# One Strassen pair for the q projection of two row chunks, in a transformer block on one Trainium2 core

## The chip, the cores and the metric

The kernel runs on one core of a Trainium2 chip. Five engines work side by side, each through its own list of instructions in order: TensorE (PE in the profile, with its weight loads as PEld), VectorE (DVE), ScalarE (ACT), GpSimd (POOL) and SyncE (SP). In this kernel SP issues most of the DMAs, POOL those of attention, and ACT a few. The metric is the device time of one execution in microseconds (us). The kernel before takes 770.53 us (median of 7 runs, 770.19 to 772.18).

## The reference

Input x has S = 2048 rows of D = 1024. Part A is a layer norm, a projection to q, k and v (1024 to 3 x 1024), a sliding attention with 32 heads of 32 (each row looks at 8 keys, two rows apart), an output projection, and a residual. Part B is a layer norm, two projections g and u to 3584, their product, and a projection down, with a residual. All data are bf16.

```python
qkv = layernorm(x) @ wqkv                  # q, k, v of 32 heads x 32
idx = pos[:, None] - 2 * arange(8)[None]   # keys s, s-2, ... s-14; before the start: masked
logits = einsum("bhsd,bhswd->bhsw", q, k[idx]) * 32 ** -0.5
o = einsum("bhsw,bhswd->bhsd", softmax(logits), v[idx])
h = x + o @ wo
n = layernorm(h)
out = h + ((n @ w_gate) * (n @ w_up)) @ w_down
```

## The kernel before

The rows are cut into four chunks of 512 (TC), numbered 0 to 3. Activations that feed a matmul are kept transposed: lnT of chunk c holds the normalised rows as 128 partitions x 8 blocks (KO) x 512. A projection group is eight matmuls of 128x128 by 128x512 into one PSUM tile. The pool of PSUM has 8 tiles.

The projection weights come in six blocks of 512 columns: blocks 0 and 1 are q, 2 and 3 are k, 4 and 5 are v. `qkv(c, blocks)` (L434) runs four groups for each block; after each group `evac_qkv` (L342) copies the PSUM tile to a staging tile on ScalarE and SP stores it to DRAM (qd, kd, vd), so that attention can load it in another layout. k and v also copy a halo of 16 rows.

Attention of one chunk (`attention`, L468) is work for VectorE: products of q and k for eight shifts, adds over the head's 32 entries, the softmax (its exponential on ScalarE), products with v, adds. It needs q and k loaded by POOL (`load_qk`, L448, L451 and L452), then v (`load_v`). At its end POOL stores o to DRAM (L536) and loads it back transposed in four parts (L539), one for each 128 rows; wo reads part t for its rows t. The four attentions run one after the other.

TensorE's order is the order of the program text. Everything else is put in between by a planner, `Background` (L37): after each group `bg.step(1.73)` adds that many microseconds of credit (times `bg.rate`, at most 4.0 in hand), and as long as credit is above zero the planner emits the next piece of the first item on its list that is due; the piece gives back its estimated VectorE time, which is taken off. An item can also ask to be called again later, which costs no credit. `bg.spend` takes credit off for VectorE work that the program emits itself, and `bg.finish` emits the rest of an item at once. Items are attention, the layer norms (`rows_gen` on VectorE for chunks 1 and 2; `NormOnScalar`, L259, on ScalarE for chunk 3), and the absolute sums of half of w_down (`abs_down`, L664: seven pieces of 128x2048 on ScalarE, each from a ring tile that ACT's queue loads), which are needed later for f16 scaling.

The stage around the change (L875 to L903): projections of chunk 0 (q, k), of chunk 1 (q, k), v of chunks 0 and 1, all of chunk 2, q and k of chunk 3; then `wo_ln2(0)` (L589), which runs the output projection of chunk 0 in eight groups, adds the residual on VectorE (L604), takes the row statistics there (L183, L184) and normalises there (L192), with the transposes on SP (L596); then v of chunk 3; then the FFN of chunk 0 (`ffn1_first`, L694), in the middle of which the output projection of chunk 1 is run by `wo_norm` (L569, matmuls L578, adds L580), whose layer norm is on ScalarE (`Norm2`, L550: sums L274, mean L277, squares L279, rstd L282 to L285, rows L296).

Weights of 1 MB stream through seven tiles (`wpool`): `pump` loads the next ones in order while fewer than seven are held, and `retire(n)` lets go of n and pumps. The ring of `abs_down` is one of the seven.

The FFN of chunks 2 and 3 is already done as Strassen pairs (`pair_block`, L829, matmuls L826): the two chunks and the two halves of the contraction, against two column blocks, give a 2x2 by 2x2 block product in seven products in place of eight. The sums of weights are in f16, scaled by a power of two that `Scale` (L628) takes from the absolute sums of the weights. The products are accumulated in PSUM, and ScalarE copies a partial sum from one PSUM tile to another (L843, L851) wherever two results share it.

## Time and profile before

| what | us |
|---|---|
| median of 7 runs | 770.53 (770.19 to 772.18) |
| the profiled execution's own time | 770.42 |
| its span, first to last instruction | 768.6 |
| TensorE busy | 763.1 (99%) |
| VectorE busy | 606.2 (79%) |
| ScalarE busy | 512.7 (67%) |
| wo of chunk 0, first matmul | 163.50 |
| FFN of chunk 0, first matmul | 191.13 |
| wo of chunk 1, first matmul | 253.29 |

The page gives busy time by engine, then the span in 40 slices of 19.2 us (a digit is the busy share in tenths), then the chain of work that ended last. A line of a list by time has start, duration, engine, line of the kernel, operation, output <- input, count, and in brackets the idle time before it with what ended it. A duration can be longer than the distance to the next instruction of the same engine, since neighbours overlap at their ends; where a sum over one engine is made, the distance from start to start is used. Granted TensorE clock is 1.00 throughout.

### The profile page before, as it was taken

To read this page: it belongs to the slowest core of one execution; us is meant where nothing else is said; L and a number is where in the kernel's file an instruction comes from. 1 tells how busy PE (TensorE), PEld (TensorE's weight loads), DVE (VectorE), ACT (ScalarE), POOL (GpSimd) and SP (SyncE) were. 2 spreads that over 40 slices of the span, in tenths; PEclk is the share of its full clock that TensorE was granted. 3 is DMA by queue.
4 is the path that set the end of the run, shared out by engine and by line. 5 is a ranking of instruction groups with operands and counts; after the bars stand their busy time and mean duration, and the time that the engine had idled before them with its cause. 6 is when DMAs were issued, how large, how long until landed. Compare 5 with 4: busy or idle time off the path is not lost.

```text
span 768.6 us, 10302 instructions
## 1 busy us (share of the span) xinstructions
PE 763.1 (99%) x3663; PEld 350.8 (46%) x3663; DVE 606.2 (79%) x718; ACT 512.7 (67%) x979; POOL 142.0 (18%) x152
## 2 busy tenths in 40 slices
PE   8999999999999999999999999999999999999998
PEld 6444444444444444444444444444444444444444
DVE  5629999999999999999998997975454444568863
ACT  4648966423687398778899986836777677788240
POOL 0000000200002000020000001018778677600000
PEclk9999999999999999999999999999999999999999
DMA  7999796999966689579559448574342423730001
GB/s 269 272 252 264 202 281 148 274 314 273 308 217 214 218 294 297 169 256 323 188 187 298 140 155 284 120 199 106 80 110 55 110 76 90 256 127 29 0 29 55
DMA packets 190915, 144.85 MB, mean 188 GB/s; under 512 B 81808, under 2 KB 181136, under 8 KB 188688
## 3 DMA queue, kind: packets, MB, share of 16 engines
q1 hardware_dynamic: 180416, 116.94, 53.8%
q0 software_dynamic: 3584, 22.02, 8.5%
q10 hardware_dynamic: 6864, 5.24, 2.4%
q8 instruction: 28, 0.46, 0.3%
q14 instruction: 23, 0.19, 0.1%
HBM read 110.10 MB, written 27.26 MB: 179 GB/s over the span
## 4 chain that ended last, share of the span: by engine, by line
PE 97%; DVE 2%; DMA 0%; issue 0%; ACT 0%; DVEq 0%
PE ps L431 21%; PE dx L944 6%; PE py L826 6%; PE pwu L431 6%; PE pg L431 6%; PE pz L826 6%; PE px L826 6%; PE pwg L431 6%; PE pu L431 6%; PE wo L998 4%; PE pv L826 3%; PE ez L944 3%; PE ey L944 3%; PE ex L944 3%; PE dy L944 3%; PE wo L578 2%
## 5 line engine op out<-in xcount | busy, mean ns | idle before, releaser
L431 PE MATMUL ps<-lnT,w_qkv 128*128 128x512 bf16 x736 | 159.5, 379 | 0.0
L431 PEld LDWEIGHTS <-w_qkv 128*128 128x128 bf16 x736 | 71.9, 98 | 86.1 <-issue 0.2
L344 ACT CAST sg<-ps 128x512 bf16<-128x512 f32 x96 | 55.1, 586 | 46.5 <-PE ps L431 41.1
L477 DVE TENSOR_TENSOR prod<-qD,kD 128x4096 bf16<-128x4096 bf16 x32 | 72.2, 2285 | 13.1 <-DMA kD<-kd 13.0
L523 DVE TENSOR_TENSOR pv<-vD,at 128x4096 bf16<-128x4096 bf16 x32 | 72.4, 2286 | 0.2
L826 PEld LDWEIGHTS <-sw 128*128 128x128 f16 x448 | 43.8, 98 | 52.9 <-issue 0.2
L431 PEld LDWEIGHTS <-w_wg 128*128 128x128 bf16 x448 | 43.8, 98 | 52.9
L431 PEld LDWEIGHTS <-w_wu 128*128 128x128 bf16 x448 | 43.8, 98 | 52.9
L826 PE MATMUL px<-lnT,ws 128*128 128x512 bf16 x224 | 55.2, 379 | 0.0
L536 POOL DMA_DIRECT2D od<-oD x4 | 2.2, 542 | 276.0 <-DVE oD L534 276.0
L431 PE MATMUL pu<-lnT,w_wu 128*128 128x512 bf16 x224 | 52.9, 379 | 0.0
L431 PE MATMUL pg<-lnT,w_wg 128*128 128x512 bf16 x224 | 52.9, 379 | 0.0
L431 PE MATMUL pwg<-lnT,w_wg 128*128 128x512 bf16 x224 | 52.9, 379 | 0.0
L431 PE MATMUL pwu<-lnT,w_wu 128*128 128x512 bf16 x224 | 52.9, 379 | 0.0
L826 PEld LDWEIGHTS <-ws 128*128 128x128 f16 x336 | 32.9, 98 | 39.6
L807 POOL TENSOR_TENSOR sw<-ws 128x512 f16<-128x512 f16 x26 | 30.0, 1154 | 82.8 <-PE pv L826 49.1
L944 PEld LDWEIGHTS <-gs 128*128 128x128 f16 (+1 forms) x280 | 27.4, 98 | 33.0
L479 DVE TENSOR_TENSOR prod<-prod 128x4096 bf16<-128x4096 bf16 x16 | 36.6, 2289 | 0.4
L843 ACT COPY py<-px 128x512 f32<-128x512 f32 x28 | 16.0, 570 | 28.6 <-PE px L826 28.6
L808 POOL TENSOR_TENSOR sw<-sw,ws 128x512 f16<-128x512 f16 x26 | 30.0, 1153 | 2.0
L810 POOL TENSOR_TENSOR sw<-ws,sw 128x512 f16<-128x512 f16 x26 | 30.0, 1154 | 0.0
L809 POOL TENSOR_TENSOR sw<-ws 128x512 f16<-128x512 f16 x26 | 30.0, 1153 | 0.0
(334 smaller groups left out, 1473.1 us busy)
## 6 DMA issues: line engine op xcount, KB each, us to landing
w_wg<-in_B_w_gate_dram SPq DMA_DIRECT2D x14, 1024.0 KB, 7.2
w_wu<-in_B_w_up_dram SPq DMA_DIRECT2D x14, 1024.0 KB, 6.4
w_pair<-in_B_w_gate_dram SPq DMA_DIRECT2D x14, 512.0 KB, 3.9
w_pair<-in_B_w_up_dram SPq DMA_DIRECT2D x14, 512.0 KB, 5.2
w_wo<-in_A_wo_dram SPq DMA_DIRECT2D x6, 1024.0 KB, 7.3
w_qkv<-in_A_wqkv_dram SPq DMA_DIRECT2D x5, 1024.0 KB, 11.3
kd<-sg SPq DMA_DIRECT2D x32, 144.0 KB, 4.3
kD<-kd POOLq DMA_DIRECT2D x4, 1152.0 KB, 8.4
```

Of the source, the lines that this page charges most:

```text
L344: nc.scalar.copy(sg[:, HB:HB + TC], ps[:])
L431: nc.tensor.matmul(ps[:], lhsT=wt[:, ko, bass.ts(j, 128)], rhs=rhs[:, ko, :], start=(ko == 0), stop=(ko == KO - 1))
L477: nc.vector.tensor_tensor(prod[:, j], qD[:], kD[:, :, o:o + SUB], ALU.mult)
L479: nc.vector.tensor_tensor(prod[:, :, 0:16], prod[:, :, 0:16], prod[:, :, 16:32], ALU.add)
L523: nc.vector.tensor_tensor(pv[:, j], vD[:, :, o:o + SUB], at[:, w, None, :].to_broadcast((128, DH, SUB)), ALU.mult)
L807: eng.tensor_tensor(sw[:, i, 0], a21, a22, ALU.add)
L808: eng.tensor_tensor(sw[:, i, 1], sw[:, i, 0], a11, ALU.subtract)
L809: eng.tensor_tensor(sw[:, i, 2], a11, a21, ALU.subtract)
L810: eng.tensor_tensor(sw[:, i, 3], a12, sw[:, i, 1], ALU.subtract)
L826: nc.tensor.matmul(ps[:], lhsT=lhs[:, ko, :], rhs=rhs[:, ko, :], start=(fresh and ko == 0), stop=(ko == 3), skip_group_check=not fresh)
L944: nc.tensor.matmul(ps[:, bass.ds(lo, n)], lhsT=lhs[k][:, bass.ts(q, 128)], rhs=rhs[k][:, bass.ds(lo, n)], start=(fresh and k == 0), stop=( ...
L998: nc.tensor.matmul(ps[:], lhsT=oTs[c][:, kk, t, :], rhs=wts["wo", 2, hf][:, kk, :], start=(kk == 0), stop=(kk == KO - 1))
```

## The change

q of chunks 2 and 3 is no longer computed by `qkv`. Blocks 0 and 1 of the weights stay in their tiles, and after wo of chunk 0 two calls of `q_pair` compute q of both chunks by seven products each for two column groups (of four). For that:

- The absolute sums of the q weights are taken during the first projections (`q_abs`, two on VectorE, two on ScalarE), one small matmul gives the scale, `q_convert` turns the two weight tiles into f16 in place, and `q_weight_sums` forms sixteen sums of weights. Since the tiles are then f16, q of chunk 1 is computed from them and scaled back in its copy.
- q of chunk 1 moves behind its k; q of chunks 2 and 3 leaves the row of projections, so wo of chunk 0 comes eight groups earlier, with v of chunk 3 ahead of it.
- `q_row_sums` forms sums of the transposed activations on VectorE, in between the adds of wo.
- In `q_pair` ScalarE makes the copies between PSUM tiles and the results of chunk 2; VectorE the results of chunk 3.
- The norm of chunk 0 after wo moves from VectorE to ScalarE, by `wo_norm(0, devs=False)`: sum and squares of each row tile in one step, the last of them, the rstd and the four rows as an item of the planner during the pair.
- q and k of chunk 0 are loaded only when the normalised rows of chunk 1 have landed (a one-element copy on POOL that reads them). The rows of chunk 3 are loaded when k of chunk 0 has landed (again by such a copy), and stand on SP ahead of two weight blocks and the transposes of chunk 2. The norm of chunk 3 is one item, due 14 us after k of the first half of chunk 1.
- `abs_down` is due 52 us after that point in place of 25 after an earlier one.
- The planner is charged 6.0 in place of 8.0 before wo. Attentions 2 and 3 are started after the pair.

The f16 view `f16` and the class `Scale` move up in the text unchanged, and `wo_ln2` is gone.

```diff
+    def f16(ap):
+        return ap.bitcast(F16)
...
-    def load_x(c, what, eng):
+    def load_x(c, what, eng, after=None):
         tiles = []
         for t in range(4):
             xt = hp.tile([128, D], BF, tag="h", name=f"{what}{c}_{t}")
+            if after is not None and t == 0:
+                nc.gpsimd.tensor_copy(xt[:, 0:1], after)
...
+            self.rstds()
+
+        def rstds(self):
...
+        def both(self):
+            yield from self.sums()
+            yield from self.rows()
...
+    scale_q = Scale("q", 4)
...
-        nc.scalar.copy(sg[:, HB:HB + TC], ps[:])
+        if c == 1 and m < 8:
+            nc.scalar.activation(sg[:, HB:HB + TC], ps[:], ACTF.Copy, scale=scale_q.inv)
+        else:
+            nc.scalar.copy(sg[:, HB:HB + TC], ps[:])
...
+                if (b, j) in at:
+                    at[b, j]()
                 ps = psum.tile([128, TC], F32, tag="mm", name=f"ps{c}_{b}_{j}")
-                mm_group(ps, wts["qkv", b], j, lnTs[c])
+                wt = wts["qkv", b][:]
+                mm_group(ps, f16(wt) if c == 1 and b < 2 else wt, j, lnTs[c])
...
-    def load_qk(c):
+    def load_qk(c, after=None):
         qD = att.tile([128, DH, SUB], BF, tag="qD", name=f"qD{c}")
         kD = att.tile([128, DH, SUB + HB], BF, tag="kD", name=f"kD{c}")
+        if after is not None:
+            nc.gpsimd.tensor_copy(qD[:, 0, 0:1], after)
...
+        def sum_dev(self, t):
+            col = slice(t, t + 1)
+            self.sum(t)
+            nc.scalar.activation(self.nm[:, col], self.s[:, col], ACTF.Copy, scale=-1.0 / D)
+            nc.scalar.activation(self.junk[:], self.xs[t][:], ACTF.Square, bias=self.nm[:, col],
+                                 accum_out=self.ss[:, col])
+
+        def finish(self, devs=True):
+            if devs:
+                yield from self.devs()
+            else:
+                yield "later", 2.0
+                self.sum_dev(3)
+                yield "later", self.pace
+                self.rstds()
+                yield "later", self.pace
             yield from self.rows()
...
-                if hf == 0 and t > 0:
+                if hf == 0 and t > 0 and devs:
                     n.sum(t - 1)
+                if hf == 1 and t > 0 and not devs:
+                    n.sum_dev(t - 1)
...
+    qsum = {}
+
+    def q_abs(k):
+        src = wts["qkv", k // 2][:, bass.ts(k % 2, 4), :]
+        if k < 2:
+            nc.vector.tensor_reduce(scale_q.l1[:, k:k + 1], src, mybir.AxisListType.XY, ALU.add,
+                                    apply_absolute_value=True)
+        else:
+            scale_q.add(k, src, att.tile([128, 4, 512], BF, tag="oT", name=f"junk_q{k}")[:])
+
+    def q_weight(r, kh, m):
+        return f16(wts["qkv", r][:, bass.ts(kh, 4), bass.ts(m, 128)])
+
+    def q_convert():
+        for r in range(2):
+            wt = wts["qkv", r]
+            nc.vector.tensor_scalar(f16(wt[:]), wt[:], scale_q.s, None, ALU.mult)
+        bg.spend(2.6)
+        bg.add(q_weight_sums(), bg.now)
+
+    def q_weight_sums():
+        for m in range(4):
+            a11, a12, a21, a22 = (q_weight(r, kh, m) for r in range(2) for kh in range(2))
+            if m < 2:
+                rooms = [f16(hp.tile([128, D], BF, tag="h", name=f"qs{m}_{i}")[:]) for i in range(2)]
+                s1, s2, s3, s4 = (r[:, bass.ts(i, 512)].rearrange("p (k c) -> p k c", k=4) for r in rooms
+                                  for i in range(2))
+            else:
+                s1, s2, s3, s4 = (t1k.tile([128, 4, 128], F16, tag="t1k", name=f"qs{m}_{i}")[:] for i in range(4))
+            nc.vector.tensor_tensor(s1, a21, a22, ALU.add)
+            nc.vector.tensor_tensor(s2, s1, a11, ALU.subtract)
+            nc.vector.tensor_tensor(s3, a11, a21, ALU.subtract)
+            nc.vector.tensor_tensor(s4, a12, s2, ALU.subtract)
+            qsum[m] = (s1, s2, s3, s4)
+            yield 1.7
+
+    def q_row_sums():
+        lo, hi = slice(0, 4), slice(4, 8)
+        b11, b21, b12, b22 = (lnTs[c][:, ks, :] for c in (2, 3) for ks in (lo, hi))
+        t1, t2, t4 = ([t1k.tile([128, TC], F16, tag="t1k", name=f"qt{i}_{k}")[:] for k in range(4)] for i in (1, 2, 4))
+        t3 = f16(b12)
+        for k in range(4):
+            nc.vector.tensor_tensor(t1[k], b12[:, k, :], b11[:, k, :], ALU.subtract)
+            nc.vector.tensor_tensor(t2[k], b22[:, k, :], t1[k], ALU.subtract)
+            if k % 2:
+                yield 1.7
+        for k in range(4):
+            nc.vector.tensor_tensor(t4[k], b21[:, k, :], t2[k], ALU.subtract)
+        yield 1.7
+        nc.vector.tensor_tensor(t3, b22, b12, ALU.subtract)
+        yield 1.3
+
+        def cells(t):
+            return [t[:, k, :] for k in range(4)]
+
+        qsum["b"] = (cells(b11), cells(b21), t1, t2, cells(t3), t4, cells(b22))
+
+    def q_product(ps, lhs, rhs, fresh):
+        for ko in range(4):
+            nc.tensor.matmul(ps[:], lhsT=lhs[:, ko, :], rhs=rhs[ko], start=(fresh and ko == 0), stop=(ko == 3),
+                             skip_group_check=not fresh)
+        bg.step(GROUP_US / 2)
+
+    def q_pair(m0, room):
+        b11, b21, t1, t2, t3, t4, b22 = qsum["b"]
+        two, inv = range(2), scale_q.inv
+
+        def bank(k, i):
+            return psum.tile([128, TC], F32, tag="mm", name=f"q{k}{m0 + i}")
+
+        def stage(c, m):
+            return t1k.tile([128, HB + TC], BF, tag="t1k", name=f"sg{c}_{m}")
+
+        def out_scalar(c, m, ps):
+            sg = stage(c, m)
+            nc.scalar.activation(sg[:, HB:HB + TC], ps[:], ACTF.Copy, scale=inv)
+            store_q(c, m, sg)
+
+        def out_vector(c, m, ps, p5):
+            sg = stage(c, m)
+            nc.vector.scalar_tensor_tensor(sg[:, HB:HB + TC], ps[:], inv, p5, ALU.mult, ALU.add)
+            bg.spend(0.75)
+            store_q(c, m, sg)
+
+        xb, yb, zb, ub, p5 = [[None] * 2 for _ in range(5)]
+        sw = [qsum[m0 + i] for i in two]
+        a11, a12, a21, a22 = ([q_weight(r, kh, m0 + i) for i in two] for r in range(2) for kh in range(2))
+        for i in two:
+            xb[i] = bank("x", i)
+            q_product(xb[i], a11[i], b11, True)
+            yb[i] = bank("y", i)
+            nc.scalar.copy(yb[i][:], xb[i][:])
+        for i in two:
+            v = bank("v", i)
+            q_product(v, sw[i][0], t1, True)
+            p5[i] = room[:, m0 + i, :]
+            nc.scalar.activation(p5[i], v[:], ACTF.Copy, scale=inv)
+            q_product(yb[i], sw[i][1], t2, False)
+            zb[i] = bank("z", i)
+            nc.scalar.copy(zb[i][:], yb[i][:])
+        for i in two:
+            q_product(zb[i], sw[i][2], t3, False)
+            ub[i] = bank("u", i)
+            nc.scalar.copy(ub[i][:], zb[i][:])
+            out_vector(3, 4 + m0 + i, zb[i], p5[i])
+            q_product(xb[i], a12[i], b21, False)
+            out_scalar(2, m0 + i, xb[i])
+        for i in two:
+            q_product(ub[i], a22[i], t4, False)
+            out_scalar(2, 4 + m0 + i, ub[i])
+            q_product(yb[i], sw[i][3], b22, False)
+            out_vector(3, m0 + i, yb[i], p5[i])
+
+    qkv(0, [1, 2], at={(1, 1): lambda: q_abs(0), (1, 2): lambda: q_abs(2), (1, 3): lambda: q_abs(1),
+                       (2, 0): lambda: q_abs(3), (2, 2): scale_q.rows})
+    qkv(0, [3], at={(3, 2): scale_q.total, (3, 3): q_convert})
+    load_qk(0, after=lnTs[1][:, 0, TC - 1:TC])
+    start_attention(0)
+    qkv(1, [2])
     bg.finish(rows2)
+    xtiles[3] = load_x(3, "x", nc.sync, after=qkv_in["k", 0][:, 0, 0:1])
+    pump(6)
+    state["live"] += 1
     for t in range(4):
         norm1[2].transpose(t)
-    xtiles[3] = load_x(3, "x", nc.sync)
-    pump(6)
-    state["live"] += 1
-    bg.add(norm1[3].sums(), bg.now + 18.0)
-    start_attention(0)
+    bg.add(norm1[3].both(), bg.now + 14.0, first=True)
     sums = abs_down()
-    bg.add(sums, bg.now + 25.0, first=True)
-    qkv(1, range(4))
+    bg.add(sums, bg.now + 52.0, first=True)
+    qkv(1, [3, 0, 1])
     qkv(0, range(4, 6))
     load_v(0)
-    bg.add(norm1[3].rows(), bg.now, first=True)
     qkv(1, range(4, 6))
     start_attention(1)
     pump(pair_at)
-    qkv(2, range(6))
-    start_attention(2)
+    qkv(2, range(2, 6))
     hss[0] = load_x(0, "h", nc.sync)
-    qkv(3, range(4), last=True)
+    qkv(3, range(2, 6), last=True)
     bg.finish(atts[0])
     bg.rate = 1.03
-    bg.spend(8.0)
-    nxt = wo_ln2(0)
-    qkv(3, range(4, 6), last=True)
+    bg.spend(6.0)
+    state["live"] += 1
+    rows_q = q_row_sums()
+    bg.add(rows_q, bg.now, first=True)
+    norm2 = [wo_norm(0, devs=False)]
+    bg.finish(rows_q)
+    room_q = wpool.tile([128, 4, TC], F32, tag="w", name="room_q")
+    norm2.append(norm2[0].finish(devs=False))
+    bg.add(norm2[1], bg.now, first=True)
+    for m0 in (0, 2):
+        q_pair(m0, room_q)
+    bg.finish(norm2[1])
+    retire(3)
+    lnT2_0 = norm2[0].lnT
+    start_attention(2)
     start_attention(3)
     norm2 = []
 
@@ -911,12 +1042,9 @@
         norm2.append(n.finish())
         bg.add(norm2[1], bg.now, first=True)
 
-    hT0 = ffn1_first(nxt[0], {(4, 2): wo_1})
+    hT0 = ffn1_first(lnT2_0, {(4, 2): wo_1})
```

## The prediction

> **What bounds the kernel now.** I read the page first (busy times, slices, chain), then the chain in order of time, then the lists of single engines around the stages that the change touches. The page, busy times and chain by engine:
>
> ```profile
> PE 763.1 (99%) x3663; PEld 350.8 (46%) x3663; DVE 606.2 (79%) x718; ACT 512.7 (67%) x979; POOL 142.0 (18%) x152
> ...
> DVE  5629999999999999999998997975454444568863
> ACT  4648966423687398778899986836777677788240
> ...
> PE 97%; DVE 2%; DMA 0%; issue 0%; ACT 0%; DVEq 0%
> ```
>
> TensorE (PE) carries 97% of the chain, so removed matmuls are time, and every stall put in between is time too. VectorE (DVE) is full from about 58 to 365 us: whatever is added there makes attention later. The chain in order of time:
>
> ```profile
> 27.09 136.41 PE ps L431 x632
> 163.50 13.81 PE wo L602 x64
> 177.31 13.81 PE ps L431 x64
> 191.13 1.73 PE pg L431 x8
> ```
>
> 136.41/632 = 0.2158 us per matmul, without a hole. The end that matters is 191.13, where the first FFN matmul starts; behind it both kernels do the same matmuls. VectorE's and GpSimd's lists, merged by time:
>
> ```profile
> 52.49 4.50 DVE L477 TENSOR_TENSOR prod<-qD,kD 128x4096 bf16<-128x4096 bf16 x2 [13.04 <-DMA kD<-kd]
> ...
> 134.44 2.29 DVE L534 TENSOR_TENSOR oD<-oD,pv 128x4096 bf16<-128x4096 bf16 x1
> ...
> 155.31 1.23 DVE L484 TENSOR_TENSOR t<-prod 128x1024 f32<-128x1024 bf16 x1
> ...
> 172.49 1.28 DVE L604 TENSOR_TENSOR h<-wo,h 128x512 bf16<-128x512 f32 x2
> ```
>
> ```profile
> 44.01 0.54 POOL L452 DMA_DIRECT2D kD<-kd  x1 [12.34 <-DMA kd<-sg]
> ...
> 137.03 0.54 POOL L536 DMA_DIRECT2D od<-oD  x1 [47.22 <-DVE oD L534]
> 141.93 3.54 POOL L539 DMA_DIRECT2D oT<-od  x4 [4.37 <-DMA od<-oD]
> ```
>
> Attention 0 waits 13.0 us for its k, then runs on VectorE without a hole of note from 52.49 to 136.73; the start of k's load sets all of it. The first wo add (172.49) comes 9 us after wo's first matmul because attention 1 was emitted ahead of it. ScalarE's (ACT) list gives the prices:
>
> ```profile
> 124.61 1.91 ACT L635 ACTIVATE w_ring<-w_ring 128x2048 bf16<-128x2048 bf16 x1
> ...
> 257.50 1.06 ACT L274 ACTIVATE njunk<-h 128x1024 bf16<-128x1024 bf16 x1 [2.97 <-DVE h L580]
> ...
> 270.75 1.15 ACT L279 ACTIVATE njunk<-h,nroom 128x1024 bf16<-128x1024 bf16 x1
> ...
> 551.16 0.57 ACT L851 COPY pz<-py 128x512 f32<-128x512 f32 x1 [0.17 <-PE py L826]
> ```
>
> Start to start on ScalarE: a sum over a row tile 1.05, its tiny mean 0.24, a square 1.15 (270.75 to 271.89); a normalised row 1.15 (280.84 to 281.97); one down sum 1.91 (124.61 to 126.52); a plain PSUM copy 0.48, a scaled one 0.59.
>
> **The change, part by part.**
>
> *Matmuls.* q of chunks 2 and 3 took 2 x 8 x 8 = 128 matmuls; seven products of 4 for each of 4 column groups are 112. Saved: 16 x 0.2158 = 3.45. The kernel has this block already: the Strassen pair blocks (L826) show 0.86 per 4 matmuls and stand in the chain without a hole, f16 weights against bf16 activations. Added: one 64-column matmul for the q scale. The like matmuls of the other scales, 512 wide, leave gaps of 0.2 to 0.3 in the chain (474.84 to 475.05); I take 0.1, between 0.03 and 0.3.
>
> *q row sums, conversion, weight sums.* Four sums over 128x2048. Two go to ScalarE at 1.91 each; they push the issue of the two chunk-1 transposes from 29.64 to about 31.7. The second of these landed 7.7 us after issue at 38.8, with q's load of 1 MB beside it, and TensorE needs it at 38.9. The change holds that load back until the transposes have landed; the others landed 3.4 to 3.8 after issue, so I expect 33.1 + 3.8 = 37. Price 0; if it takes 7.7 again, 40.8, it costs 1.9. Two go to VectorE. No such reduction is in the trace; by size it lies between the 2048-element bf16 add (1.23) and four bn_stats (4 x 0.64 = 2.56), and I take 2.3, the 2 x 1.2 of a 1024-element f32 add. VectorE is idle from 18.00 to 20.43 and from 22.83 to 24.96, exactly where they land, so at 2.3 they cost attention nothing, and at 2.56 about 0.4 us of a row that is not yet due. [...] Conversion is 2 x 1.28 (128x4096), the weight sums 16 x 0.34 (14 f16 subtractions of 512 took 4.78): 8.0 us from about 40, done by 48.5, under the 13 us wait for k. Without that cover all 8.0 would fall on attention 0.
>
> *k's load, x3, SP's queue.* The last k store follows ScalarE, about 1.5 us later than now, so kD is issued at 45.5 instead of 44.0. (On POOL only qD and kD stand behind the new copy that waits for the transposes, and nothing until 88 behind the one that waits for kD.) It landed in 8.4 beside four transposes and x3. These now stand behind it, and the same-sized vD load at 88.24 took 6.4, od (1024 KB) 4.6. I take 5.8: landing at 51.3 against 52.4, so attention 0 is 1.1 earlier (bounds 4.6 and 8.4: 2.3 earlier to 1.5 later). SP now waits for kD before x3, and behind x3 stand the two w_qkv loads, the chunk-2 transposes and the k stores of chunk 1. w_qkv 4 was issued at 49.1 and took 11.3; now about 54.5 + 11.3 = 65.8, needed at 66.6. Price 0, upper end 2. ScalarE's chunk-3 sums wait for ln tiles held by those transposes, some 2 us, covered by eight PSUM banks (8 x 1.73 = 13.8 us). Chunk 3's transposes now stand among chunk 0's last v stores on SP; the last is issued near 84.4, lands in 3.0, so vD is loaded at 88 as now (88.24) and lands 6.4 later, at 94.6, needed at 100. Price 0.
>
> *wo earlier.* Eight projection groups less stand ahead of wo(0): it starts at 163.50 - 13.81 + 0.1 = 149.8. Its first transposed output landed at 141.9 + 5.5 = 147.4; with attention 0 1.1 earlier, 146.3. 3.5 us in hand.
>
> *VectorE at wo.* Following the planner's credits by hand to the 76th group, attention 1 has been given all but the last adds of its second block, so VectorE reaches the first wo add where L484 at 155.31 ends now, 156.6, less 1.1: 155.5. The q row sums (12 x 0.34 and one of 128x2048, 1.2) are emitted from the sixth add on; the part that v needs is done at about 165, when v is due at 165.3, the last (t3) near 168, z at 168.8: price 0 here, and 1:1 once VectorE is later than 157. Chunk 0's statistics (4 x 2.0) leave VectorE; 16 small subtractions and eight PSUM outputs (0.67 each) come: about 2.7 net, so attention 1 ends near 240 instead of 237.0. Its wo starts at 253.3 and the first oT landed at 248.2, so 2 us remain.
>
> *ScalarE at wo and in the pair.* Here the gain goes. Four sum-and-square steps of 2.44 (9.8), two down sums that the new due time puts at 162 and 174 (3.8), the small rstd group (1.33), four rows (4.6): 19.5, besides 24 copies (12.8), between 156.8 and the pair's end. In order of emission: adds of row 0 done at 156.8; sums 0, 1, 2 to 164.2; sixth down sum to 166.1; only then the first x-to-y copy, 166.7. TensorE's y0 could start at 166.2: stall 0.55. Then p5, z0, the fourth sum-and-square (168.1 to 170.6), p5, z1 copy to 171.8: z1 product stalls 0.76. u0 copy behind the rstd group: 0.08. Row 0 and the seventh down sum delay an output: the second pair's v stalls 0.14; row 1 ahead of its first copy: y0 stalls 1.35; rows 2 and 3: 0.11 and 0.49. Together 3.5.
>
> *End of the pair.* Row 3 is done at 184.9; its transpose landed in 3.2 at 185.9 and in 8.1 at 282.1. So 188.1 to 193.0 against 191.3: price 0, upper end 1.7.
>
> **Sum.** 770.42 (profiled execution: span 768.6 and 1.8 around it; 0.1 under the median 770.53) - 3.45 + 0.1 + 3.5 = 770.6. The FFN starts at 191.3, where it starts now.
>
> **The rivals.**
>
> *Faster: ScalarE keeps up.* If the two down sums fall into the gaps of wo rather than into the pair, the same row of stalls shrinks to z1 0.76, u0 0.08, z1 0.18: 1.0, time 770.42 - 3.35 + 1.0 = 768.1. For it: ScalarE was idle 2 to 3 us at a time in wo(1) (2.97 at 257.50). Against it: the planner's credit is below zero there, -7 after the finish of attention 0 and the charge of 6, so it cannot emit them. Without any stall: 767.1.
>
> *Slower: k lands late.* kD needs 8.4 as now: landing 53.9, wo's adds from 158.1, and every microsecond after 154.9 goes one for one into the first y copy. 770.42 - 3.35 + 2.93 + 3.2 = 773.2. It decides beyond 772.1, that is k landing later than 52.8. For it: SP's stores run beside it. Against: x3, weights and transposes no longer do.
>
> *A transfer is late.* The chunk-1 transpose, w_qkv 4, or chunk 0's last transpose: 1 to 2 us each, 771.6 to 772.6.
>
> *VectorE ends attention 1 too late.* 240 + 11.2 (od issue to first oT, as now) = 251.2 against 253.5; an od store of 4 more us costs 2: 772.6.
>
> **How the numbers follow.** About 0.2% (1.5 us) is what a measurement of this kernel tells from no change. Forecast (769.0 to 772.1): 0.42. ScalarE keeps up, below 769.0: 0.24. Late k: 0.18; late transfer: 0.10, half of it over 772.1; attention 1 late: 0.06. Faster 0.24; same 0.42 + 0.05 = 0.47; slower 0.18 + 0.05 + 0.06 = 0.29. The range goes from 768.0 (rival, 768.1) to 774.0 (late k with one late transfer); the forecast alone 769.0 to 772.1.
>
> **What would show it.** Matmuls 3663 - 15; the FFN's first matmul near 191.3; waits of TensorE on ScalarE's copies between 163 and 191 that add up to 3.5, the largest at the second pair's y0; kD landing near 51.3; first wo add near 155.5; w_ring sums inside the pair. I am wrong if TensorE shows no waits there (faster), or waits before 150 or at 253 (slower).

## The result, and the profile after

The changed kernel takes 774.83 us (median of 17 runs, 771.85 to 778.71) where the kernel before takes 770.67 on the same chips: a ratio of 1.005, 95% interval 1.0035 to 1.0065. The prediction was 770.6, its range 768.0 to 774.0. The change is slower, by about 4 us.

These runs fall into groups by the TensorE clock that was granted. Seven are at 1.000 and lie at 771.9 to 773.2; ten are at 0.998 or 0.996 and lie at 774.4 to 778.7. The kernel before was at 1.000 in all eleven executions whose clock is listed with the first set of experiments. (The trace of sums32 below has a granted clock of 0.57 over 4 us and 1.00 on both sides, which makes 3.4 us at half clock. One such window costs 1.7 us, 0.2% of 773, so 0.998 fits one and 0.996 two.) So two things are to be explained: 2.6 us at full clock, and the lower clock.

The profiled execution is one at full clock: 773.08 us, span 771.3 (before: 770.42, span 768.6). Its page, busy times, slices and chain by engine:

```profile
PE 761.7 (99%) x3648; PEld 349.3 (45%) x3648; DVE 625.8 (81%) x750; ACT 535.5 (69%) x1013; POOL 145.1 (19%) x154
...
DVE  6789999989999999999998999885554444568863
ACT  4755957589677398778899985836777676788240
...
PE 64%; DVE 20%; ACT 9%; DMA 4%; issue 2%; ACTq 0%; SPq 0%; DVEq 0%; POOLq 0%
```

TensorE has 3648 matmuls, 15 fewer, as meant, but it no longer carries the chain alone: 97% has become 64%. From the first FFN matmul back, the chain now runs through ScalarE in the pair, then through VectorE's attention 1 and attention 0. TensorE's own list shows where it waits (start, time, in brackets the idle time before and what ended it):

```profile
150.98 13.99 PE L648 MATMUL wo<-w_wo,oT 128*128 128x512 bf16 x64 [1.20 <-DMA oT<-od]
...
167.78 1.02 PE L939 MATMUL qy<-qt,qs 128*128 128x512 f16 x4 [0.22 <-ACT qy L971]
...
173.09 1.02 PE L939 MATMUL qz<-lnT,qs 128*128 128x512 f16 x4 [0.84 <-ACT qz L979]
...
182.41 1.02 PE L939 MATMUL qy<-qt,qs 128*128 128x512 f16 x4 [1.16 <-ACT qy L971]
...
187.38 1.02 PE L939 MATMUL qz<-lnT,qs 128*128 128x512 f16 x4 [0.34 <-ACT qz L979]
...
192.56 1.89 PE L482 MATMUL pg<-lnT,w_wg 128*128 128x512 bf16 x8
...
501.76 10.52 PE L1072 MATMUL ez<-t,a22r 128*128 128x512 f16 x48 [1.02 <-DVE hsr L789]
```

Three places: the first output projection waits 1.20 for the first transposed output of attention 0; the pair waits four times for ScalarE's copies; and at 501.76, deep in the output of the first layer, TensorE waits 1.02 for VectorE. None of the three is in the kernel before. Between the pair's first matmul (164.80) and the first FFN matmul (192.56) lie 27.76 us, of which 28 products take 24.17 (28 x 0.8633), so the pair loses 3.6: the 2.56 in brackets, 0.17 more at each of the four (the brackets count from the end of the last matmul, the sum from start to start), and 0.4 in three gaps that are too small for a bracket.

ScalarE's list in the pair shows why, and GpSimd's list shows the loads and stores of attention:

```profile
165.26 1.90 ACT L362 ACTIVATE w_ring<-w_ring 128x2048 bf16<-128x2048 bf16 x1
167.06 0.19 ACT L362 ACTIVATION_READ_ACCUMULATOR w_ring<-w_ring 128x1 f32 x1
167.15 1.05 ACT L971 COPY qy<-qx 128x512 f32<-128x512 f32 x2
...
177.60 1.90 ACT L362 ACTIVATE w_ring<-w_ring 128x2048 bf16<-128x2048 bf16 x1
...
180.63 1.24 ACT L304 ACTIVATE ln<-h,nroom,rs 128x1024 bf16<-128x1024 bf16 x1
181.77 0.59 ACT L971 COPY qy<-qx 128x512 f32<-128x512 f32 x1
```

```profile
46.07 0.54 POOL L508 DMA_DIRECT2D kD<-kd  x1 [8.62 <-DMA kd<-sg]
...
92.45 0.53 POOL L513 DMA_DIRECT2D vD<-vd  x1 [37.99 <-DMA vd<-sg]
...
136.57 0.54 POOL L592 DMA_DIRECT2D od<-oD  x1 [42.56 <-DVE oD L590]
144.43 3.54 POOL L595 DMA_DIRECT2D oT<-od  x4 [7.32 <-DMA od<-oD]
```

Two down sums of 1.90 stand in the pair ahead of copies that TensorE waits for, as forecast. A new fact is in the last line: the store of attention 0's output was waited for 7.32 us (before: 4.37), and the first transposed output landed at 150.98, where TensorE was ready at 149.78.

| step, us | before | forecast | after |
|---|---|---|---|
| load of k issued | 44.01 | 45.5 | 46.07 |
| attention 0 starts | 52.49 | 51.3 | 52.12 |
| load of v issued | 88.24 | 88 | 92.45 |
| output of attention 0 stored | 137.03 | 135.9 | 136.57 |
| first wo matmul | 163.50 | 149.8 | 150.98 |
| first wo add on VectorE | 172.49 | 155.5 | 156.01 |
| first FFN matmul (chain) | 191.13 | 191.3 | 192.72 |
| span | 768.6 | 768.8 | 771.3 |

The 2.7 us of span are 1.6 up to the first FFN matmul and the wait of 1.0 near 501. The chain in order of time shows what sets the 1.6:

```profile
151.28 2.30 DVE prod L535
...
156.01 1.29 DVE h L650 x2
...
157.32 1.16 ACT njunk L279 x2
...
165.35 1.40 ACT w_ring L362
...
167.25 0.96 ACT qy L971 x2
...
186.74 0.60 ACT qz L979
...
187.38 1.02 PE qz L939 x4
```

VectorE is in attention 1 until 156.01, only then makes the first add of wo, and ScalarE works from 157.32 to the pair's last copies with hardly a pause. The wait of 1.20 at wo(0) is not on this chain: had TensorE been on time there, it would have waited 1.2 longer for the first of ScalarE's copies. In this execution, then, the 1.6 come by way of ScalarE, and the wait at wo(0) would count only if it were longer.

### The profile page after: what moved, and what is told of

Same layout as the page of the kernel before. It is cut to its first block, busy times and chain, and to the rows that moved or that the text cites. A ratio compares the mean times of both kernels' runs of the same rounds, so it can differ in the third digit from the quotient of the medians.

```text
span 771.3 us, 10350 instructions
## 1 busy us (share of the span) xinstructions
PE 761.7 (99%) x3648; PEld 349.3 (45%) x3648; DVE 625.8 (81%) x750; ACT 535.5 (69%) x1013; POOL 145.1 (19%) x154
## 4 chain that ended last, share of the span: by engine, by line
PE 64%; DVE 20%; ACT 9%; DMA 4%; issue 2%; ACTq 0%; SPq 0%; DVEq 0%; POOLq 0%
PE dx L1072 6%; PE px L831 6%; PE pwg L482 6%; PE pu L482 6%; PE py L831 6%; PE pz L831 6%; PE pwu L482 6%; PE pg L482 6%; DVE prod L533 3%; PE pv L831 3%; DVE pv L579 3%; PE dy L1072 3%; DMA b21r<-in_B_w_down_dram 2%; DVE prod L535 2%; PE wo L648 2%; PE wo L1126 2%
## 5 line engine op out<-in xcount | busy, mean ns | idle before, releaser
L482 PE MATMUL ps<-lnT,w_qkv 128*128 128x512 bf16 x608 | 131.7, 379 | 0.0
L482 PEld LDWEIGHTS <-w_qkv 128*128 128x128 bf16 (+1 forms) x608 | 59.3, 98 | 70.9
L396 ACT CAST sg<-ps 128x512 bf16<-128x512 f32 x72 | 41.7, 586 | 27.1 <-PE ps L482 14.6
```

Of the source, the lines that this page charges most:

```text
L396: nc.scalar.copy(sg[:, HB:HB + TC], ps[:])
L482: nc.tensor.matmul(ps[:], lhsT=wt[:, ko, bass.ts(j, 128)], rhs=rhs[:, ko, :], start=(ko == 0), stop=(ko == KO - 1))
```

## The experiments

**Theory at the start.** At full clock the pair loses its gain to ScalarE, the first output projection waits for a slow store, and the end loses 1.0 to VectorE. The lower clock comes from short waits of TensorE. Rivals: the clock spread is the chip's; the waits are VectorE's or those of short staging tiles.

**Does it come again?** No edit.

> The changed kernel once more, nothing edited. Seventeen executions of it fell into three groups: granted clock 1.000 at 771.9 to 773.2, 0.998 at 774.4 to 776.0, 0.996 at 777.0 to 778.7, where the kernel before stays at 770.1 to 771.7. Theory (short waits of TensorE let the clock drop to half for a window of some 3.4 us): the groups come again, at least a third of the executions are below 1.000, and if the profiled execution is one of them its half-clock window opens within 5 us behind one of the waits of 0.8 us or more (first transposed output near 150, pair's y products near 171 and 180, output products near 501). Rival (the spread is the chip's, not the kernel's): on another occasion all executions are at 1.000 and the median is near 773.0.

777.27 us (4 runs; 1.0089, 1.0074 to 1.0104): one at 772.88 and clock 1.000, one at 776.35 and 0.998, two at 778.2 to 778.4 and 0.996; eleven runs of the kernel before beside it are all at 1.000. So the spread is the kernel's. The profiled execution was the one at full clock (wait at wo(0) 1.79, near 501 0.49), so where a half-clock window stands could not be seen in it; the half clock and the 3.4 us of the theory were first shown by the trace of sums32 below. wo(0) starts 0.58 later in it than in the first profile, but the first add of wo (156.35) and the first FFN matmul (192.90) both come 0.34 later: the FFN's start follows VectorE and ScalarE, not wo(0).

**Which waits lower the clock?** In the kernel before, two kernels with waits put in by hand:

```diff
+ if j == 1 and b < 4:            # one group in each of four gate blocks
+     ... matmuls ko = 0..3 ...
+     nc.scalar.copy(pg[:], pg[:])             # before_waits: once
+     for _ in range(b + 2): nc.scalar.copy(pg[:], pg[:])   # before_longer instead
+     ... matmuls ko = 4..7 ...
```

> The kernel before, with four waits put in by hand: in the second group of the first four gate blocks of chunk 0's FFN, ScalarE copies the half-summed PSUM bank onto itself between the fourth and the fifth matmul. The result is the same and nothing else moves. Each holds TensorE for 0.8 to 1.4 us. Theory (a short wait of TensorE is enough for a half-clock window): 770.6 + 4 x 1.2 = 775.4 in executions at full clock, and a good part of the executions at 0.998 or less and 1.7 to 4 us above that. Rival (the half-clock windows come from something else in the change): every execution at 1.000, all of them within 1 us of 775.4.

> As the four waits put into the kernel before, but with two, three, four and five in-place copies of the PSUM bank in the gate blocks 0 to 3: waits of TensorE of about 1.7, 2.3, 2.9 and 3.4 us. Four waits of up to 1.3 us left the clock at 1.000 in every execution. Theory (a wait of more than some 2 us lets the clock fall to half for one window of 3.4 us): clock 0.998 to 0.993, windows behind the longest two or three waits, 770.5 + 10.3 + 1.7 for each window: 782.5 to 786. Rival (not the length of a wait, but something of the change's own traffic): clock 1.000 in all executions, 780.8.

Waits of 1.08 to 1.25 us: 775.68, within 0.05 us in four runs, all at 1.000. Waits up to 3.5 us: 784.64 (783.12 to 785.91), the four executions at 0.993, 0.998, 0.993 and 1.000. TensorE's list and the stretches around the four waits of the second kernel (columns: us, busy time and count of PE, PEld, DVE, ACT, POOL; granted clock; DMA share; GB/s):

```profile
197.38 1.02 PE L721 MATMUL pg<-lnT,w_wg 128*128 128x512 bf16 x4 [1.86 <-ACT pg L720]
...
213.64 1.02 PE L721 MATMUL pg<-lnT,w_wg 128*128 128x512 bf16 x4 [2.28 <-ACT pg L720]
...
230.50 1.87 PE L721 MATMUL pg<-lnT,w_wg 128*128 128x512 bf16 x4 [2.88 <-ACT pg L720]
...
250.92 1.86 PE L721 MATMUL pg<-lnT,w_wg 128*128 128x512 bf16 x4 [3.49 <-ACT pg L720]
```

```profile
190.00:200.00 10.00, 8.14 (x39) 3.62 (x38) 8.38 (x13) 4.67 (x10) 0.00 (x0) 1.00 1.10 309
206.00:216.00 10.00, 7.72 (x36) 3.42 (x35) 9.93 (x7) 7.00 (x13) 0.00 (x0) 1.00 0.91 288
222.00:232.00 10.00, 7.12 (x31) 3.00 (x29) 8.74 (x6) 7.18 (x14) 0.00 (x0) 0.88 0.78 260
...
246.00:252.00 6.00, 2.51 (x10) 0.96 (x9) 5.01 (x4) 4.74 (x11) 0.54 (x1) 0.85 1.08 368
```

Waits of 1.86 and 2.28 left the clock at 1.00, those of 2.88 and 3.49 did not, and the four matmuls behind them took 1.87 instead of 1.02. So my first form of the theory, that a wait of about 1 us is enough, is wrong; in this trace 2.88 and 3.49 us were enough, though not always: the execution at 1.000 (783.54) has the same four waits built in. In the two profiles of the changed kernel the wait at wo(0) is the longest, and it varies (1.20, 1.79); the pair's longest is 1.16 in both.

**The down sums out of the pair.**

```diff
- bg.add(sums, bg.now + 52.0, first=True)
+ bg.add(sums, bg.now + 32.0, first=True)
```

> The down sums are due 32 us behind the start of chunk 1's projections instead of 52, so that none of the seven is emitted inside the pair or the stretch of wo; nothing else is edited. Theory (the pair's stalls are ScalarE's queue): the stalls of the second pair's y product (1.16) and of the last z (0.34 to 0.2) fall away and the first pair's z1 (0.8) stays; the first FFN matmul comes 1.5 to 1.7 earlier than 192.7, and with two loads of 512 KB less beside it the output store of chunk 0 lands sooner than 7.3 us, for up to 1.2 more. Time at full clock 773.0 - 1.6 = 771.4, down to 770.2 with the store. Rival (the stalls come from VectorE or from PSUM banks, not from ScalarE's down sums): the stalls stay at 2.6 and the time at 773.

774.11 us (6 runs, 771.4 to 775.3; 1.0039). The pair's part came as the theory had it: only the first pair's z1 (0.84) is left. But a down sum now stands ahead of attention 0's exp (VectorE waits 3.31 for it instead of 1.1), attention 0's output is issued at 139.02 instead of 136.57, and the gain goes into the wait at wo(0). TensorE's waits, and the stretches around wo(0), of this profiled execution:

```profile
PE wo L648 <- DMA oT<-od: 3.1, 2, 2.9
PE ez L1072 <- DVE hsr L789: 1.8, 1, 1.8
...
PE qz L939 <- ACT qz L979: 0.8, 1, 0.8
```

```profile
148.00:153.00 5.00, 2.07 (x11) 0.75 (x10) 4.93 (x5) 1.28 (x4) 2.29 (x3) 1.00 1.16 248
153.00:157.00 4.00, 4.00 (x12) 1.47 (x11) 3.93 (x3) 0.00 (x0) 0.00 (x0) 0.57 1.08 328
157.00:161.00 4.00, 4.00 (x20) 1.85 (x19) 3.29 (x5) 1.21 (x3) 0.00 (x0) 1.00 1.09 349
```

Here is a half-clock window in place: behind a wait of 2.9, 12 matmuls in 4 us at a granted clock of 0.57, then 20 at 1.00. In stretches of 2 us from 152 the clock is 0.87, 0.50, 0.78 and 1.00, that is 3.4 us at 0.50.

**The q projections as plain groups.**

```diff
- for m0 in (0, 2):
-     q_pair(m0, room_q)
+ for c in (2, 3):
+     qkv(c, [0, 1])        # on the scaled f16 weights; row sums left out
```

> The q projections of chunks 2 and 3 stay behind wo of chunk 0 but are 16 plain groups of 8 matmuls each on the same scaled f16 weights; the q row sums and the x-to-y-to-z copies are left out, all else stays. 16 matmuls more, 3.45 us. Theory (the pair saves 3.45 and loses 2.6 of it to ScalarE): no stall of TensorE between 151 and the first FFN matmul, which comes near 151.0 + 13.8 + 27.6 = 192.4, where the changed kernel has 192.7; VectorE has some 10 us less to do, so attention 3 ends earlier and the wait of 1.0 near 501 goes: 771.8 at full clock, and if the half-clock windows come from the pair's waits, fewer executions with them. Rival (the rest of the move, not the pair, costs the time): 3.4 more than the changed kernel, 776.4.

786.3 us (4 runs), clock 0.996 to 0.989, and no verdict on the pair: the last transposes for the FFN took 16.4 us beside attention 1's loads, and TensorE waited 10.1 for them. What it does show is the clock without any pair: half-clock windows at a wait of 2.5 near 115 (ScalarE held for 13.3 us by late v stores; granted clock 0.91, 0.50 and 0.73 in the stretches of 2 us from 114) and at that of 10.1 (the 8 matmuls behind it take 3.57 instead of 1.73), and none at the wait of 1.2 at wo(0) (5 matmuls in 1.25).

**Is v's load the cause?** In the changed kernel two of chunk 3's transposes stand on SP between chunk 0's last v stores and wait there for the lnT buffer.

```diff
- bg.add(norm1[3].both(), bg.now + 14.0, first=True)
+ bg.add(norm1[3].sums(), bg.now + 14.0, first=True)
  ...
  load_v(0)
+ bg.add(norm1[3].rows(), bg.now, first=True)
```

> One part of the change undone: chunk 3's normalised rows and transposes are given out behind the load of chunk 0's v again, its row sums stay where the change put them. In the changed kernel two of these transposes stand on SP's queue between chunk 0's last v stores and wait there until chunk 0's last projection frees the lnT buffer: v's load is issued at 92.45 (before: 88.24), lands in 7 to 12 us, and the same congestion holds ScalarE for 8 to 13 us near 102 on staging tiles. Theory (this delay is what makes the output of attention 0 late and TensorE wait): v's load is issued 2 to 4 us earlier, near 89, attention 0 never waits for it, od0 is issued at 136.3 in every execution, TensorE's wait at wo(0) stays at 1.2 or less, and the executions at 0.998 and 0.996 become fewer than one third: median near 773. Rival (the output store itself is slow, 7 us beside 2 MB of weights): the wait at wo(0) keeps its 1.2 to 2.9 and the clock groups stay as they are.

774.65 us (6 runs, 772.8 to 778.62; 1.0056). v's load is issued at 89.20, as expected, but attention 0's output is issued at 137.46, its store is waited for 8.22, TensorE waits 3.57 at wo(0), and a window follows (7 matmuls in 3.17, where 8 take 1.89 at full clock). Moving v's load does not help: the rival held.

**Are the staging tiles short?** In the kernel before, 8 of the 30 held:

```diff
+ held = [t1k.tile([128, HB + TC], BF, tag="t1k", ...) for i in range(8)]
+ for t in held: nc.gpsimd.memset(t[:, 0:1], 0.0)
  load_qk(0)
  ...                              # read by GpSimd behind wo(0)
```

> The kernel before, in which 8 of the 30 staging tiles are held by a marked byte from the load of chunk 0's q to the end of the first output projection, as the change holds them for the weight sums of column groups 2 and 3; nothing else is edited. Theory (22 staging tiles are too few when the three loads of 3.3 MB fill the DMA engines near 92 to 105): ScalarE's longest wait for a staging tile grows from 3.6 to 8 us or more, and where it passes some 13 us TensorE waits for a bank: up to 3 us, in some executions with a half-clock window: 771 to 776. Rival (the tiles are not short, the stores are late for another reason): 770.5 as before, ScalarE's longest wait stays under 5.

770.71 us (10 runs; 1.0005, 0.9996 to 1.0014). ScalarE's longest wait for a tile stays at 3.6. In the kernel before, at least, the tiles are not short.

**Three edits at once**: the rows behind v's load, the down sums at 32, and in the first layer's output

```diff
  if q == 1:
+     load_down(b21, 1, 0)
      load_h1(a22, 1, parts=(1,))
      nc.sync.dma_start(hsr1[:], hsd[1][:])
-     load_down(b21, 1, 0)
```

> Three edits to the changed kernel: chunk 3's rows behind the load of chunk 0's v, the down sums due at 32 us instead of 52, and in the first layer's output the reload of the lower down weights issued ahead of the second part of the h reload and of the residual. Theory: v's load near 89, wait at wo(0) 1.2 or less, pair's stalls about 1.0 instead of 2.7, no wait of the output products near 501 (1.0 before): 773.1 - 1.7 - 1.0 - 0.5 = 769.9 with the clock at 1.000 in most executions, which is 0.6 under the kernel before. Rival (the jam near 92 to 105 only moves): wait at wo(0) 2 to 3 with half-clock windows, 772 to 775.

779.44 us (4 runs; 1.0116), worse than the changed kernel. At wo(0) 3.52 and a window (7 matmuls in 3.00). Near 500 the reload of the down weights lands in 9.2 instead of 14.4, but the h reload behind it takes 12.0 instead of 8.7, VectorE waits 4.2 for that, and TensorE waits 2.06 with a second window (granted clock 0.62 from 506.7 to 511.2):

```profile
506.74 5.52 PE L1073 MATMUL ez<-t,a22r 128*128 128x512 f16 x17 [2.06 <-DVE hsr L789]
```

**What slows the store?** In the kernel before, 2 MB of loads put where the changed kernel has its weight loads:

```diff
- qkv(2, range(6))
+ extra = [t1k.tile([128, HB + TC], BF, tag="t1k", ...) for i in range(16)]
+ qkv(2, range(5)); extra_load(0)          # 8 x 128 KB of the output weights
+ qkv(2, [5]);      extra_load(1)
```

> The kernel before, with 2 MB of weights loaded a second time, into 16 idle staging tiles that nobody reads: 1 MB ahead of the last v block of chunk 2 (near 129) and 1 MB ahead of chunk 3's first projection (near 136). That is about where the changed kernel has its two output-projection weight loads; the kernel before has its own near 145, behind the store of attention 0's output. Theory (the store of attention 0's output takes 7 us instead of 4.4 because the change puts these loads beside it): the store lands in 6 us or more instead of 4.4; the time stays at 770.5, since there the output projection starts only at 163.5. Rival (the store is slow for another reason): it lands in 4.4 to 5.

773.6 us (6 runs, 771.85 to 776.41; 1.0038). The store is waited for 5.20 instead of 4.37: less than expected. (The first megabyte was issued from 130.27, the second from 138.13, just behind the store; the changed kernel's two loads of the output weights stand at 130 and 137.) The time, which I had put at no change, rose, since the loads also hold back the output weights (TensorE waits 1.4) and the FFN's transposes (2.3). Then I cleared the changed kernel's window in three steps:

```diff
  # ring_oT
- ring = wpool.tile([128, KO, 512], BF, tag="w", name="w_ring")
+ ring = att.tile([128, KO, 512], BF, tag="oT", name="w_ring")
- yield "later", 4.9 * GROUP_US            # between two down sums
+ yield "later", 3.3 * GROUP_US
- bg.add(sums, bg.now + 52.0, first=True)
+ bg.add(sums, bg.now + 40.0, first=True)
- pump(pair_at)                            # ahead of chunk 2
+ pump(7); state["limit"] = 8              # behind chunk 2; the rest behind attention 0
  ...                                      # the rest of the sums at the end of attention 0
  # ring_rows: ring_oT, and chunk 3's rows behind load_v(0)
  # clean: ring_rows, and pump(7), load_x(0) moved up into chunk 2's k blocks
```

> The changed kernel with the traffic ahead of the output of attention 0 thinned out: the down weights' ring lies in the room of the transposed output, which is empty until then, all seven down sums are given out between chunk 2's k and chunk 3's v (due at 40 us, 5.7 us apart), the slot that this sets free takes the first half of the output weights near 122, the second half follows near 130, and the first FFN weights wait until attention 0 is given out. Theory (the wait at wo(0) is the output store beside 2 MB of weights and 1.5 MB of down weights): the store lands in 4.4 to 5.5 instead of 6.6 to 8.2, TensorE's wait at wo(0) is 0.5 or less, the pair's stalls are about 1.0, the clock stays at 1.000 in most executions: 773.1 - 1.2 - 1.7 = 770.2, with 0.5 to 1 more where the wait near 501 grows. Rival (the store is slow whatever stands beside it, or attention 0 ends late because ScalarE's exp waits behind a down sum): wait of 1 to 3 and half-clock windows, 772 to 776.

> As the kernel with the ring in the transposed output's room, and chunk 3's rows behind the load of chunk 0's v, so that this load is issued near 89 instead of 92. Theory: attention 0 never waits for v, so the executions spread less; 770.2 at the median as without it, or 0.3 less. Rival (the order of the stores near 90 matters more than v's load, and attention 0 ends near 137.5 as with the rows alone): 0.5 to 1 more than without it.

> The kernel with the ring in the transposed output's room and chunk 3's rows behind v's load, with the two loads that still stood beside attention 0's output store there moved further up: the first half of the output weights in the middle of chunk 2's k (near 107 instead of 129), the residual's rows behind it (near 112 instead of 130); only the second half of the output weights remains, near 131 to 134. Theory (the store of attention 0's output is slow because the change has pushed 1 MB of rows, 2 MB of weights and the down weights' loads into the 14 us that wo(0) was moved up): the store lands in 4.4 to 5.5, TensorE waits 0.5 or less at wo(0), fewer than a quarter of the executions show a half-clock window, median 770.5 to 771.2. Rival (the small k and v stores of chunk 3 are what slows it): 6.5 to 8, wait 1.5 or more, 772 to 774.

| kernel | DMA share in the 13 us ahead of the store | store waited for, us |
|---|---|---|
| before | 0.35 | 4.37 |
| before_load2 | 0.49 | 5.20 |
| after, and again | 1.00, 1.03 | 7.32, 7.21 |
| sums32 | 1.08 | 6.63 |
| rows_later | 1.05 | 8.22 |
| ring_oT | 0.98 | 8.15 |
| ring_rows | 0.96 | 7.40 |
| clean | 1.21 | 9.20 |

ring_oT 774.64 us (6 runs), ring_rows 773.14 (12 runs, 770.89 to 775.97; 1.0033, 1.0021 to 1.0045), clean 774.65 (6 runs). The three thin the pair's stalls to 0.84 as expected, but the store stays slow in all of them, in clean too, where the theory was 4.4 to 5.5. ring_rows also shows what the pair's stalls are worth. TensorE's list:

```profile
151.78 13.99 PE L648 MATMUL wo<-w_wo,oT 128*128 128x512 bf16 x63 [2.08 <-DMA oT<-od]
...
191.09 1.89 PE L482 MATMUL pg<-lnT,w_wg 128*128 128x512 bf16 x8
```

wo(0) starts 0.8 later than in the changed kernel, and still the FFN starts 1.5 earlier (192.56 there). Its six executions at full clock have a median of 771.86, the changed kernel's seven 772.93. Back to the store: the versions that are not in the table lie at 7.2 to 9.6 with shares of 0.97 to 1.10; among the full stretches the share does not order the waits. (The share adds up the times of all packets, so it can pass 1.00.) The fixed stretch from 124 to 137, first of the kernel before, then of the changed one, then of clean:

```profile
124.00:137.00 13.00, 13.00 (x62) 5.85 (x60) 12.83 (x7) 9.46 (x26) 0.00 (x0) 1.00 0.35 87
```

```profile
124.00:137.00 13.00, 13.00 (x62) 5.90 (x61) 12.83 (x7) 8.19 (x20) 0.42 (x1) 1.00 1.02 274
```

```profile
124.00:137.00 13.00, 13.00 (x62) 5.93 (x61) 12.86 (x6) 11.25 (x31) 0.00 (x0) 1.00 1.22 288
```

In the kernel before the DMA engines are two thirds idle there (87 GB/s); the rows of x, the output weights and the rest come behind the store, since wo(0) starts at 163.50. The change moves wo(0) up by 13 us, and what has to be there before it moves with it, into a stretch that also has the k and v stores. Taking single loads out did not empty it: SP was late, and others took their place (in ring_oT the first output weights and the rows of x, given out near 122, were issued at 130 to 135; in clean three loads of down weights and eleven stores of k and v stand there). That a full stretch goes with a slow store is what the table shows; that one kind of transfer is to blame is not shown, the small k and v stores included, and two megabytes alone are not enough.

**Is VectorE a second bound?** One kernel gives it more work, one takes TensorE's saving alone, one takes the row sums away.

```diff
  # before_dve4, attention 2, first block: each product twice
+ for _ in range(2 if c == 2 and wp == 0 else 1):
      nc.vector.tensor_tensor(prod[:, j], qD[:], kD[:, :, o:o + SUB], ALU.mult)
  # before_less16, four q groups of chunk 3: ko in range(4) instead of 8
  # no_rowsums, changed kernel: the pair's t1..t4 are raw halves of the rows
```

> The kernel before, in which attention 2 carries out its first two products of q and k twice, the same values into the same tile: 4.6 us more of VectorE ahead of attention 3, nothing else. In the changed kernel attention 3's output is stored 4.9 later than before and TensorE then waits 0.5 to 1.0 near 501 for VectorE, behind a reload of the lower down weights of 13 to 16 us instead of 9 to 11. Theory (the later end of attention 3 is enough for that): output of attention 3 stored near 463, the reload 13 us or more, a wait of 0.5 to 1.5 near 499: 771 to 772. Rival (the wait comes from TensorE's own shift): no wait, 770.5.

> The kernel before with 16 matmuls left out and nothing put in: the four q groups of the upper heads of chunk 3 sum only the first four of their eight products (so their values are half sums). That is what the change saves on TensorE, 3.45 us, without its price. My prediction took it that behind the first FFN matmul both kernels run alike, so that TensorE's gain would reach the end. Theory A (that step holds): no new wait of TensorE, 770.5 - 3.45 = 767.1. Theory B (VectorE, full to about 465 us, ends just in time for the output products near 410 to 501; 4.6 us more on it gave a wait of 3.7 there): a wait of 2 to 3 near 410 or 501 takes back what VectorE does not follow; at most 0.5 to 1.5 of the 3.45 reaches the end, 769.0 to 770.0, and where the wait passes 2 us a half-clock window adds 1.7.

> The changed kernel without the row sums of the pair on VectorE: its products take the raw halves of the rows instead of the four sums (q of chunks 2 and 3 come out as other values; matmuls, copies and stores are the same). 5.3 us less on VectorE ahead of attention 1's rest. Theory B (VectorE is the second bound): the wait near 501 (0.5 to 1.0) goes, attention 3's output is stored near 459 to 460; the wait at wo(0) and the pair's stalls stay: 0.5 to 1.0 less, 772.2 at full clock, the clock groups as in the changed kernel. Rival (the wait near 501 is the reload's alone): no change, 773.0.

before_dve4: 775.9 us (4 runs; 1.0071), the profiled one 774.37 at 1.000, the others at 0.997 and 0.998. No wait near 499; instead one of 3.7 at 410.67, ahead of the first layer's scale, for a sum on ScalarE, and TensorE is 3.7 later from there on. So VectorE has about 0.9 us in hand there (4.6 less 3.7), but the run doesn't tell whether attention 3's end makes the wait near 501. before_less16: 768.85 us (11 runs; 0.9975, 0.9966 to 0.9983): of 3.45 us, 1.7 reach the end. The rest is lost at the FFN's start, which neither theory had; the waits of TensorE in that kernel:

```profile
PE pg L431 <- DMA lnT<-ln: 1.6, 1, 1.6
...
PE l1psh L650 <- DVE rowbh L645: 0.2, 1, 0.2
```

In the kernel before, chunk 0's transposed rows for the FFN land just in time; TensorE can be at most some 1.8 us earlier without more work on them. no_rowsums: 775.62 us (6 runs); the three at full clock take 773.1 to 773.3, not less than the changed kernel's 771.9 to 773.2. So VectorE's 5.3 us of row sums are not what the changed kernel loses; that theory falls. Its profiled execution (779.7) has the store at 9.60, a wait of 5.66 at wo(0), one of 3.10 at the pair's z1, and a half-clock window at each (from start to start, wo's 64 matmuls take 15.15 instead of 13.8, and the three products from 181.90 on 1.28, 1.70 and 1.30 instead of 0.86).

**Is the wait at wo(0) the one that lowers the clock?** Keep TensorE at work through it:

```diff
+ fill = psum.tile([128, TC], F32, tag="mm", name="fill")
+ for i in range(12):
+     nc.tensor.matmul(fill[:], lhsT=ones[:], rhs=lnTs[3][:, 0, :], start=True, stop=True)
  norm2 = [wo_norm(0, devs=False)]
```

> The changed kernel with 12 matmuls that nobody reads (2.6 us, on operands that have long been there) ahead of wo(0): TensorE works while it would wait for the first transposed output. Theory (the half-clock windows that most executions of the changed kernel show open behind that wait, when it passes about 2 us): the wait that is left is 2 or less in every execution, no window near 153, four fifths of the executions or more at 1.000; time 773.0 + 2.6 - 1.2 to 2.6 = 773.0 to 774.4 with a median near 773.7, that is lower than the 774.8 without these matmuls although there is more work. Rival (the windows come from the pair, or from the end): the clock groups stay, 774.5 to 780, median near 776.

> The same 12 matmuls ahead of wo(0) in the kernel with the ring in the transposed output's room and chunk 3's rows behind v's load, the nearest to the kernel before so far (770.9 to 772.6 at full clock, half of its executions with a window). Theory: full clock in four fifths of the executions, 771.7 + 2.6 - 2.1 = 772.2 at the median, with a spread of 1 us; not below the kernel before. Rival: windows as without, 773 to 776.

filler: 774.03 us (5 runs, 772.98 to 774.81), all five at 1.000, where the same kernel without these matmuls had 13 of 21 below it. ring_filler: 772.24 (12 runs, 771.64 to 775.57; 1.0026, 1.0017 to 1.0036), eleven of twelve at 0.999 or more, where ring_rows had six. TensorE's list of filler:

```profile
149.37 2.75 PE L1025 MATMUL fill<-lnT,ones 128*128 128x512 bf16 x12
151.96 4.26 PE L648 MATMUL wo<-w_wo,oT 128*128 128x512 bf16 x19
```

With 2.6 us more of work the median is lower by 0.8 us, and in the ring kernel by 0.9; the ratios to the kernel before overlap in their intervals (1.0026 to 1.005 against 1.0035 to 1.0065, 1.0017 to 1.0036 against 1.0021 to 1.0045), so the gain in time is not clear of noise. The clock is: with the wait filled, nearly all executions stay at full clock. So the windows of the changed kernel come from the wait at wo(0), all but few. No version of the change beats the kernel before.

## Why the prediction was wrong

- *Matmuls, scale, row sums of the weights, conversion*: right. 3648 matmuls; the two sums on VectorE took 2.23 and 2.28 (forecast 2.3) in the holes named.
- *k's load*: right to 0.8. Issued at 46.07, landed in 5.9 (5.8), attention 0 starts at 52.12. The rival of a late k did not come.
- *"vD is loaded at 88 as now"*: wrong. It was issued at 92.45. Two of chunk 3's transposes are given out ahead of chunk 0's last two v stores and wait on SP for the buffer of lnT that chunk 0's last projection frees. It landed at 99.7, and attention 0's first product with v starts at 101.92 without a wait, so it cost nothing in the profiled execution; putting it back to 89.20 gained nothing either.
- *ScalarE in the pair*: the mechanism was right, the size too small, and the match of 3.5 forecast with 3.6 measured is luck. The stalls are at y0, z1, y0 and z1, the largest at the second pair's y0, as forecast, and with the two down sums gone (sums32, ring_rows) the listed waits fall from 2.56 to 0.84. But TensorE came to the pair 1.2 late. The copy for the first y0 would have come no sooner had it been on time, and the pair would have lost about 4.8 (an estimate, 3.6 and 1.2). Where the forecast fell short: row 0 was done at 157.3, not 156.8, and the first three sum-and-square steps took 7.9 up to the down sum (157.32 to 165.26), not 7.4. One step is 2.69 from start to start (157.32 to 160.01) where the forecast had 2.44: the rows that it was priced from have other instructions behind them (a copy starts 1.14 after a square there, 270.75 to 271.89; here the next sum starts 1.27 after it, 158.74 to 160.01). So the first y0 starts at 167.78, not 166.75, and the FFN at 192.6, not 191.3.
- *"3.5 us in hand" at wo(0)*: this step failed. It took the store's 4.4 and the transposed load's 5.5 from a trace in which the DMA engines were 35% busy ahead of them. After the move they were full: store 7.3, load 6.5, together 3.9 more, and attention 0's end came 0.7 later than forecast. 3.5 in hand became 1.2 short at best (in the profiles of the changed kernel 1.2 and 1.8, in those of its versions up to 5.7). A wait before 150 was the prediction's own sign of a slower result, and it came. At full clock ScalarE's delay covers it; its price is the clock, below. I had priced a slow output store, but for attention 1 alone.
- *"Behind it both kernels do the same matmuls"*: wrong by 1.0, the wait near 501 (0.4 to 2.1 in the changed kernel and most of its versions, absent in the kernel before). Attention 3's output is stored 4.9 later, 1.6 of which are TensorE's. Its cause stays open: reordering the reload made it worse, and before_dve4 put its wait elsewhere.
- *The clock*: not in the prediction at all. In the profiles the waits of 2.9 us and more at wo(0) (2.9 to 5.66, in six versions of the change) were each followed by a window at half clock, those of 1.20, 1.79 and 2.08 were not; a window of 3.4 us, as in sums32, is about 1.7 us more. In 10 of 17 executions the clock is lower; the longer wait and its window together are what moves the median from 773 to 774.8, as filler and ring_filler show for the clock.
- *The faster rival* had the pair's stalls at 1.0 and 768.1. sums32 and ring_rows have those stalls, yet no execution came under 770.8. The slower outcome came by a late transfer, a rival that I gave 0.10 and in which I had listed three others.

The sum at full clock, along TensorE's list: 770.42 - 3.35 + 3.6 + 1.2 + 1.0 = 772.9, against 773.08 measured. Read by causes, the 3.6 and the 1.2 are one term, ScalarE's 4.8 in place of 3.5. So of the 4.2 us between forecast and median, 1.3 are the mis-sized ScalarE term, 1.0 the wait near 501, and the rest, some 1.9, is put down to the long waits at wo(0) with their windows.

## What to carry to other kernels

A transfer time read from a trace holds for the traffic that stood beside it there: the same store took 4.37 us behind a stretch with a DMA share of 0.35, and 7.32 behind one of 1.00. When a change moves a stage up, list what must land before it, and look at the DMA share of the stretch into which all that moves; a stage moved up by 13 us needs its loads 13 us earlier too. And look at the granted clock around a wait of TensorE: in these traces waits of up to 1.86 us left it at 1.00, those of 2.5 us and more, all but one, came with one or two windows at half clock, some 1.7 us each beyond the wait's own length, and 12 matmuls that do nothing (2.6 us) kept the clock at 1.000 in five of five executions at no loss of time (774.03 against 774.83). Two waits in a row on one engine can also hide one another: before a wait is counted as a loss, ask whether the engine would only have waited further on.
